# A reciprocal on VectorE in place of an exponential and two products, with the order of a planned kernel worked out anew

## The chip, the cores and the metric

The kernel runs on one core of one Trainium2 chip. The metric is device time in microseconds (us). The engines are TensorE (PE in the profile, with PEld for its weight loads), VectorE (DVE), ScalarE (ACT), GpSimd (POOL) and SyncE (SP, which issues the DMAs). They run beside each other, each works through its own list of instructions strictly in order, and they wait for each other by semaphores.

## The reference

A linear attention with a complex decay per step, followed by a two-layer network with a softplus. Sizes are batch B=4, heads H=8, sequence S=768, head dimension D=48, d_model 384, d_ff 2048; all fp32.

```
mag = sqrt(a_re^2 + a_im^2);  scale = min(mag, 0.999) / (mag + 1e-6)
for t in range(S):                       # per batch and head, S_re and S_im are D x D
    S_re, S_im = ar*S_re - ai*S_im + k_t v_t^T,  ar*S_im + ai*S_re      # (ar, ai) = a*scale
    y[t] = q_t . S_re
x = y, as B*S tokens of 384
out = softplus(x @ w_in) @ w_out
```

The kernel before does not step through t. It takes the logarithm of the decay: log(mag) from log(a_re) and 0.5*log(1 + r^2), and the angle from arctan(r), where **r = a_im/a_re** is the ratio of the decay's two parts. Both are summed along the sequence, and q and k are multiplied by exp(+-sum), cos and sin, so that chunks of 128 steps become matmuls.

## The kernel before

The sequence is cut into 6 groups of 128 steps, a group has 4 chunks (one for each batch), 24 chunks in all. The decay's work (the function `pre`) is done in 14 slices: slices 0 to 3 are one chunk of group 0 each, 128x384 elements; slices 4 to 13 are two chunks each, 128x768 elements. For a slice, `pre` lists these steps in this order:

- DMAs bring a_re, a_im (`x`, the parts `re()` and `im()`) and q, k into one buffer.
- L466 to L471 make the ratio r in `v3`: on ScalarE `v1 = Ln(re)` and `v2 = Exp(-v1)`, which is 1/re to the precision of two table functions, and on VectorE three products, the last two of which correct it: `im = im*v2`, `v3 = re*v2`, `v3 = (v3 - 2)*im`. This is -r, so that the arctan further down takes it with scale -1.
- L473 to L481 make log(mag) with its cap, on ScalarE (Square, Ln, Exp, Ln) and VectorE (L476, L481).
- The running sums along the sequence: in slices 0 to 3 by a matmul with a triangular mask (`sums`, L507), in the others by VectorE's scan (`scan`, L486 to L493). Then exponentials (L525, L526), the product with q and k (L530), arctan (L532), angles (L545, L547), sine and cosine (L535 to L537) and two products with q and k (`tail`, L563, L565).

For each chunk, `chunk` moves q and k into the layout `qk` by DMA, transposes k (L621, L628, L630), computes scores (L646), masks them on VectorE (L649), multiplies by v and by the state (L677, L680) and splits the result y in two fp32r parts, high `xt0` (L688 on VectorE or L689 on ScalarE) and low `xt1` (L690, VectorE). `kv` (L701) and L707 to L710 update the state.

The network (`moe`) runs for 512 tokens of one group and 128 columns of d_ff at a time, in 96 such steps. A step is nine matmuls into `h` (L736), on ScalarE Abs, Exp and Ln (L741 to L743), on VectorE `lt = max(h,0) + lt` (L744), a high part `gh` (L746 on VectorE or L747 on ScalarE, whichever the planner picks), a low part `gl` (L748, VectorE), and, two steps later in the list, nine matmuls into three `o` accumulators (L760). Two buffers `h`, two `lt` and six `g` lie between the engines. The weights are converted from words of 64 bits on VectorE and ScalarE (L350 to L367).

The order of all this is not written by hand. Every step is added to a `Planner` with an engine, a duration that the planner assumes, and a key; `order` then plays the engines through with these assumed durations, and at each moment takes the step with the lowest key that is ready. The keys come from a table of numbers `K`. Steps with an alternative (`gh`, `xt0`, copies of `o`, some conversions) go to the engine that the planner finds free. Where TensorE would have nothing to do before the first `o` matmul is planned, the planner puts in filler matmuls (L796) whose result is not used. The assumed durations are formulas, for example:

```
def d1(n):
    return n / 960 + 0.066
def a1(n, ap=0):
    return n / 1200 + 0.1 + 0.09 * ap
```

Of the kernel before, what the change touches and what calls it, by code (L numbers as in the profile page):

```python
# [15 lines left out]
AF = mybir.ActivationFunctionType  # L16
ALU = mybir.AluOpType
# [67 lines left out]
class Planner:  # L85
# [29 lines left out]
    def add(self, eng, dur, fn, key, r=(), w=(), tab=None, nbytes=0):  # L115
        t = Task(eng, dur, fn, key, len(self.tasks), tab, nbytes)
        self.tasks.append(t)
        seen = set()
        for accs, wr in ((r, False), (w, True)):
            for a in accs:  # L120
                buf, part = a if isinstance(a, tuple) else (a, None)
                for e in buf.hist:
                    if (part is None or e[0] is None or e[0] == part) and (wr or e[2]) and e[1] is not t:
                        t.deps.add(e[1])
                if wr and part is None:
                    buf.hist = []
                buf.hist.append((part, t, wr))
                if buf not in seen:
                    seen.add(buf)
                    buf.users += 1  # L130
                    t.bufs.append(buf)
        return t
# [128 lines left out]
def d1(n):  # L261
    return n / 960 + 0.066
# [6 lines left out]
def a1(n, ap=0):  # L269
    return n / 1200 + 0.1 + 0.09 * ap  # L270
# [6 lines left out]
class Prog:  # L277
# [119 lines left out]
    def pre(self, si):  # L397
        nc = self.nc
        V, A, PE = nc.vector, nc.scalar, nc.tensor
        add = self.plan.add  # L400
# [3 lines left out]
        W = n * CH  # L404
# [9 lines left out]
        if first:  # L414
            ra, ia, sa = [(x, (z, 0))], [(x, (z, 2))], [(x, (z, 1))]
        else:
            ra, ia, sa = [(x, (0, 0))], [(x, (1, 0))], [(x, (0, 1)), (x, (1, 1))]
# [3 lines left out]
        if first:  # L421
            t = Buf(self.wpool, f"w{'io'[si % 2]}{NWP - 1 - si // 2}", [P, 2 * NI * WCOL], F32R, f"t_{si}")
            t1, t2, t3 = (((t, j), lambda j=j: t()[:, j * W : (j + 1) * W].bitcast(F32)) for j in range(3))
            t4, t5 = t2, t1
        else:
            t1, t2, t3, t4, t5 = ((z, lambda z=z: z()[:, :W]) for z in
                                  (Buf(p, "t", [P, 2 * NI * CH], F32, f"t{j}_{si}", NT) for j in range(1, 6)))
# [4 lines left out]
        def region(j):  # L432
            return x().rearrange("p (c j n) -> p c j n", c=2, j=2)[:, z : z + m, j]

        if first:
            re = lambda: region(0)[:, 0, :W]
            im = lambda: region(0)[:, 0, W:]
        else:
            re = lambda: region(0)[:, 0]
            im = lambda: region(0)[:, 1]  # L440
# [6 lines left out]
        col = lambda j: chk[:, 2 * si + j : 2 * si + j + 1]  # L447
# [3 lines left out]
        def at(part="head"):  # L451
            step[0] += 1
            return K[part][si] + step[0] * 0.05
# [6 lines left out]
        for c in range(m):  # L460
# [2 lines left out]
            add("SP", 0.45, lambda vt=vt, gc=gc: nc.sync.dma_start(vt(), self.vpad[:, gc, :]),  # L463
                K["chunk"][gc] - K["vlead"], w=[vt], nbytes=4 * VW * P)

        add("ACT", a1(W), lambda: A.activation(v1(), re(), AF.Ln), at(), r=ra, w=[t1], tab="log")  # L466
        add("ACT", a1(W, 1), lambda: A.activation(v2(), v1(), AF.Exp, scale=-1.0, accum_out=col(0)),
            at(), r=[t1], w=[t2, (self.flags, 2 * si)], tab="log")
        add("DVE", d1(W), lambda: V.tensor_tensor(im(), im(), v2(), ALU.mult), at(), r=[t2], w=ia)
        add("DVE", d1(W), lambda: V.tensor_tensor(v3(), re(), v2(), ALU.mult), at(), r=[t2] + ra, w=[t3])  # L470
        add("DVE", d1(W), lambda: V.scalar_tensor_tensor(v3(), v3(), 2.0, im(), ALU.subtract, ALU.mult),  # L471
            at(), r=ia, w=[t3])
        add("ACT", a1(W, 1), lambda: A.activation(re(), v3(), AF.Square, accum_out=col(1)),  # L473
            at(), r=[t3], w=ra + [(self.flags, 2 * si + 1)])
        add("ACT", a1(W, 1), lambda: A.activation(re(), re(), AF.Ln, bias=self.one), at(), w=ra, tab="log")
# [45 lines left out]
        else:  # L521
            lb, vl = t1, v1
            add("DVE", st, lambda: scan(0, v1, v1), at(), r=[car[0]],
                w=[t1] + ([(self.flags, (0, si))] if last else [car[0]]))
# [4 lines left out]
            keep(0, lb, vl, at())  # L529
        add("DVE", d1(2 * W), lambda: V.tensor_tensor(region(1), region(1), region(0), ALU.mult), at(), r=ca, w=sa)  # L530
        def arctan():
            A.activation(v3(), v3(), AF.Arctan, scale=-1.0)  # L532

        def sincos():
            A.activation(v4(), v3(), AF.Sin, scale=TURN)  # L535
# [22 lines left out]
        def tail():  # L558
            h = NI * 2 * CH
            for c in range(m):  # L560
# [5 lines left out]
                    at("tail"), r=[t4], w=r1)  # L566

        return (arctan, a1(W), [t3]), (sincos, 2 * a1(W) + a1(W, 1) + 0.28, [t4, t3]), turn, tail

    def trig(self, key, *parts):  # L570
# [384 lines left out]
    def tokens(self):  # L955
# [75 lines left out]


K = {
    "judge": 1000000.0,
    "head": [
        274.27, 191.42, -19.05, 1886.88, -522.94, 3908.76, 1353.27, 120.66, 663.62, 2137.45, 3530.29,
        1964.06, 1785.73, 1014.39,
    ],
    "turn": [
        -811.22, 2808.33, 895.09, 2597.24, -283.88, 1643.47, 2180.8, 1352.75, 1602.08, 2955.2, 3052.45,  # L1040
        2418.74, 2757.83, 1578.39,
    ],
    "tail": [
        -2437.59, 1540.19, -1353.87, 2017.89, -135.23, 668.85, 932.44, 944.77, 145.34, 194.8, 232.6,
        1598.99, 1138.83, 2676.38,
    ],
    "chunk": [
        -689.49, -686.77, 740.28, 1628.59, 1541.82, 611.66, 1299.05, 1015.66, 1529.3, 1799.41, 3880.02,
        3677.37, 1662.92, 1429.47, 2231.74, 1027.09, 2317.51, 356.29, 1181.0, 2433.8, 429.57, 324.71,
        492.66, 2147.0,  # L1050
    ],
    "state": [
        -865.61, -1248.14, -159.16, -396.04, 43.1, 43.1, 90.73, 46.85, 128.01, 128.32, 139.34, 139.15,
        154.61, 198.54, 235.65, 212.71, 254.45, 273.15, 303.36, 280.34, 880.92, 864.29, 16.84, 1017.82,
    ],
    "wgt": [
        -474.48, -2074.48, -586.01, -122.47, -914.3, 393.73, -1500.13, 949.7, 1718.07, 1958.85, 814.56,
        993.07, 2739.59, 1078.09, 309.09, 77.07,
    ],
    "moe": [  # L1060
        38.3, 81.85, 155.32, 196.13, 296.48, 341.98, 532.78,
    ],
    "step": [
        4.721, 3.356, 1.527, 6.239, 2.402, 18.243, 113.085,
    ],
    "seen": 258.893,
    "seenstep": 56.443,
    "rlead": -1133.562,
    "xlead": -906.378,
    "vlead": 57.841,  # L1070
    "plead": -233.471,
    "backlog": 1.833,
    "altpen": -0.192,
    "tpen": 10.673,
    "table": 1.3,
}

# [61 lines left out]
```

## Time and profile before

| | |
|---|---|
| median of 3 runs | 598.09 us (597.23 to 829.45) |
| the profiled execution, its own time | 598.15 us |
| its span, first to last instruction | 596.4 us |
| TensorE busy | 577.3 us (97%) |
| VectorE busy | 439.0 us (74%) |
| ScalarE busy | 437.3 us (73%) |
| granted TensorE clock | 0.997 |

The page gives busy times over the whole span, and these are averages over an opening, in which slices are prepared and TensorE runs mostly filler, and a long stretch in which the network's matmuls run. A busy TensorE may be running filler: the 328 records of L796 are the 164 filler instructions, each recorded as two passes, and they hold TensorE for 39.8 us.

### The profile page before, as it was taken

What the parts mean: (1) busy time and instruction counts of PE and PEld (TensorE: products, weight loads), DVE (VectorE), ACT (ScalarE), POOL (GpSimd) and SP (SyncE); (2) the same over time, 40 slices, a digit from 0 to 9 for tenths busy, and PEclk for the clock granted to TensorE, in tenths of its full rate; (3) what the DMA queues carried; (4) which work ended last, traced back from release to release, by engine and by line L of the source; (5) the groups of instructions that cost most, each with busy time, mean ns of one, the idle gap of its engine ahead of it and who ended that gap; (6) DMA issues with size and microseconds to landing.
All of it is one profiled execution on the core that took longest, in us unless ns stands there. A gap on an engine that the chain in (4) does not pass through costs nothing.

```text
span 596.4 us, 10864 instructions
## 1 busy us (share of the span) xinstructions
PE 577.3 (97%) x4338; PEld 487.0 (82%) x4338; DVE 439.0 (74%) x678; ACT 437.3 (73%) x768; POOL 1.8 (0%) x16
## 2 busy tenths in 40 slices
PE   1999999999999999999999999999999999999995
PEld 1999988888878888888888888887888888888884
DVE  6999999998998989777876985979336643533442
ACT  7987587847988695948859769687458834569982
POOL 1000000000000000000000000000000000000000
PEclk9999999999999999999999999999999999999998
DMA  8899843404004345515440435414105600057712
GB/s 324 343 301 276 316 123 123 123 27 165 0 1 106 124 114 183 138 53 159 102 143 28 130 129 130 144 51 106 43 1 158 175 2 1 1 153 243 217 50 57
DMA packets 42232, 75.47 MB, mean 127 GB/s; under 512 B 3520, under 2 KB 26560, under 8 KB 42176
## 3 DMA queue, kind: packets, MB, share of 16 engines
q1 hardware_dynamic: 42176, 74.73, 41.1%
q8 instruction: 35, 0.57, 0.4%
q14 instruction: 21, 0.17, 0.1%
HBM read 50.33 MB, written 5.51 MB: 94 GB/s over the span
## 4 chain that ended last, share of the span: by engine, by line
PE 80%; DVE 7%; ACT 7%; DMA 2%; SPq 1%; issue 1%; ACTq 0%; DVEq 0%
PE o L760 29%; PE h L736 28%; PE o L796 6%; PE sc L646 6%; PE kv L701 3%; PE y L680 3%; PE y L677 2%; PE tr L621 1%; DMA x<-dense_dram 1%; ACT L848 1%; DVE lt L744 1%; PE sum L507 1%; SPq L606 1%; ACT lt L742 1%; DVE gl L748 1%
## 5 line engine op out<-in xcount | busy, mean ns | idle before, releaser
L736 PE MATMUL h<-xt,wi 128*128 128x512 f32 x864 | 217.5, 397 | 0.2
L760 PE MATMUL o<-gh,wo 128*128 128x512 f32 x576 | 198.2, 400 | 0.0
L736 PEld LDWEIGHTS h<-xt,wi 128*128 128x128 f32 x864 | 159.7, 188 | 36.3 <-DVE lt L744 1.0
L744 DVE SCALAR_TENSOR_TENSOR lt<-h,lt 128x512 f32<-128x512 f32 x96 | 66.0, 688 | 93.1 <-ACT lt L743 92.9
L760 PEld LDWEIGHTS o<-gh,wo 128*128 128x128 f32 x576 | 108.4, 188 | 25.9 <-issue 1.8
L760 PE MATMUL o<-gl,wo 128*128 128x512 f32 x288 | 113.6, 395 | 0.0
L741 ACT ACTIVATE lt<-h 128x512 f32<-128x512 f32 x96 | 56.7, 592 | 77.1 <-PE h L736 74.0
L743 ACT ACTIVATE lt<-lt,one 128x512 f32<-128x512 f32 x96 | 69.2, 721 | 1.9
L748 DVE TENSOR_TENSOR gl<-lt,gh 128x512 fp32r<-128x512 f32 x96 | 66.2, 689 | 5.7 <-ACT gh L747 3.6
L760 PEld LDWEIGHTS o<-gl,wo 128*128 128x128 f32 x288 | 54.3, 188 | 11.5 <-DVE gl L748 0.4
L742 ACT ACTIVATE lt<-lt 128x512 f32<-128x512 f32 x96 | 60.4, 629 | 1.9
L646 PE MATMUL sc<-qk 96*128 96x128 f32 x384 | 49.1, 278 | 0.5 <-DVE xt L690 0.4
L646 PEld LDWEIGHTS sc<-qk 96*128 96x128 f32 x384 | 46.7, 192 | 2.8 <-PE sc L646 0.6
L649 DVE TENSOR_TENSOR a<-sc,mask 128x512 f32<-128x512 f32 x48 | 32.2, 684 | 12.6 <-PE sc L646 12.6
L796 PE MATMUL o<-ident 128*128 128x128 f32 x328 | 39.8, 278 | 0.0
L796 PEld LDWEIGHTS o<-ident 128*128 128x128 f32 x328 | 38.5, 194 | 0.2 <-issue 0.2
L747 ACT ACTIVATE gh<-lt 128x512 fp32r<-128x512 f32 x38 | 23.9, 629 | 19.8 <-DVE lt L744 16.5
L490 DVE TENSOR_TENSOR_SCAN t<-hold,t 128x384 f32<-128x384 bf16 x40 | 36.1, 945 | 1.2 <-DMA out_dram<-o 0.3
L848 ACT ACT_TABLE_LOAD x28 | 35.9, 1283 | 0.4
L701 PEld LDWEIGHTS kv<-v,kt 128*96 128x96 f32 x320 | 29.6, 165 | 2.0 <-ACT kt L628 0.5
L701 PE MATMUL kv<-v,kt 128*96 128x64 f32 (+1 forms) x320 | 29.7, 246 | 0.0
L563 DVE TENSOR_TENSOR x<-x,t 128x768 f32<-128x768 f32 x24 | 22.0, 952 | 10.6 <-ACT t L537 10.4
(88 smaller groups left out, 617.5 us busy)
## 6 DMA issues: line engine op xcount, KB each, us to landing
x<-dense_dram SPq DMA_DIRECT2D x20, 768.0 KB, 5.9
qk<-x SPq DMA_DIRECT2D x48, 288.0 KB, 4.2
raw_wo<-w_out_dram SPq DMA_DIRECT2D x8, 768.0 KB, 9.0
raw_wi<-w_in_dram SPq DMA_DIRECT2D x8, 768.0 KB, 10.1
seen<-w_in_dram SPq DMA_DIRECT2D x16, 384.0 KB, 3.8
seen<-w_out_dram SPq DMA_DIRECT2D x16, 384.0 KB, 3.7
v<-vpad_dram SPq DMA_DIRECT2D x24, 224.0 KB, 2.6
qk<-x SPq DMA_DIRECT2D x48, 96.0 KB, 3.8
```

The lines of the kernel that those rows point to most:

```text
L490: V.tensor_tensor_scan(out()[:, s], self.hold, inc()[:, s], 0.0, ALU.mult, ALU.add)
L646: PE.matmul(psc()[:, hh * P : (hh + 1) * P], q[:, h, CH:], q[:, h, :CH], start=True, stop=True)
L701: PE.matmul(kv()[: 2 * D, s], k[:, 2 * D * h : 2 * D * (h + 1)], v[:, s], start=h == 0, stop=h == H - 1)
L736: PE.matmul(h()[:, :n], w()[:, q, i, fs], x()[:, i, :n], start=k == 0, stop=k == 3 * NI - 1)
L741: add("ACT", a1(n) - 0.04, lambda: A.activation(tv(), h(), AF.Abs), k, r=[h], w=[t])
L742: add("ACT", a1(n), lambda: A.activation(tv(), tv(), AF.Exp, scale=-1.0), k, w=[t], tab="log")
L743: add("ACT", a1(n, 1), lambda: A.activation(tv(), tv(), AF.Ln, bias=self.one), k, w=[t], tab="log")
L744: add("DVE", d1(n), lambda: V.scalar_tensor_tensor(tv(), h(), 0.0, tv(), ALU.max, ALU.add), k, r=[h], w=[t])
L748: add("DVE", d1(n), lambda: V.tensor_tensor(gl(), tv(), gh().bitcast(F32), ALU.subtract), k, r=[t, gh], w=[gl])
L760: PE.matmul(acc[m]()[:, :n], w()[:, wq, f % 2, ms], x(), start=f == f0 and q == 0, stop=f == f1 - 1 and q == 2)
L796: self.nc.tensor.matmul(self.acc0[0]()[:, :P], self.ident, x, start=True, stop=True)
L848: nc.scalar.preload_act_table_set(TABLES[table])
```

## The change

In `pre`, 1/re comes from VectorE's reciprocal instruction and is multiplied once by im. The Exp and two of the three products go. The Ln of re stays, since log(mag) needs it; it moves behind the two VectorE steps in the list, and it now carries the sum over columns (`accum_out`) that the Exp carried. The ratio has its natural sign, so the arctan loses its scale of -1. The planner assumes `d1(W)` for the reciprocal, the same as for a product. From L466 on, line numbers of the changed kernel are lower by 3 (L744 becomes L741), except within the changed lines.

```diff
-        add("ACT", a1(W), lambda: A.activation(v1(), re(), AF.Ln), at(), r=ra, w=[t1], tab="log")
-        add("ACT", a1(W, 1), lambda: A.activation(v2(), v1(), AF.Exp, scale=-1.0, accum_out=col(0)),
-            at(), r=[t1], w=[t2, (self.flags, 2 * si)], tab="log")
-        add("DVE", d1(W), lambda: V.tensor_tensor(im(), im(), v2(), ALU.mult), at(), r=[t2], w=ia)
-        add("DVE", d1(W), lambda: V.tensor_tensor(v3(), re(), v2(), ALU.mult), at(), r=[t2] + ra, w=[t3])
-        add("DVE", d1(W), lambda: V.scalar_tensor_tensor(v3(), v3(), 2.0, im(), ALU.subtract, ALU.mult),
-            at(), r=ia, w=[t3])
+        add("DVE", d1(W), lambda: V.reciprocal(v2(), re()), at(), r=ra, w=[t2])
+        add("DVE", d1(W), lambda: V.tensor_tensor(v3(), im(), v2(), ALU.mult), at(), r=ia + [t2], w=[t3])
+        add("ACT", a1(W, 1), lambda: A.activation(v1(), re(), AF.Ln, accum_out=col(0)),
+            at(), r=ra, w=[t1, (self.flags, 2 * si)], tab="log")
...
-            A.activation(v3(), v3(), AF.Arctan, scale=-1.0)
+            A.activation(v3(), v3(), AF.Arctan)
...
 K = {
...
     "head": [
-        274.27, 191.42, -19.05, 1886.88, -522.94, 3908.76, 1353.27, 120.66, 663.62, 2137.45, 3530.29,
...
+        -189.5437767, -1095.6183614, 1348.051687, 4369.562575, -1151.1824664, 4502.4467243, 1094.3014723,
...
-    "altpen": -0.192,
-    "tpen": 10.673,
+    "altpen": 1.1854543,
+    "tpen": 0.0,
```

All the keys in `K` are new, so all engines' lists are in another order. Counted over the whole list, `gh` is now made on VectorE 87 times and on ScalarE 9 times (58 and 38 before), the high part of y on VectorE 15 times and ScalarE 9 (8 and 16), copies of `o` on VectorE never and on ScalarE 18 times (7 and 11). There are 149 fillers (164 before). The list still has 28 table loads on ScalarE.

VectorE's list at the start of the program, where slices 0 and 1 (buffer `x_98`, work tiles `t_105` and `t_110`) and slice 2 (`x_101`, `t_116`) are begun, before:

```order
L469 TENSOR_TENSOR x_98<-x_98,t_105 128x384
L470 TENSOR_TENSOR t_105<-x_98,t_105 128x384
L471 SCALAR_TENSOR_TENSOR t_105<-t_105,x_98 128x384
L469 TENSOR_TENSOR x_98<-x_98,t_110 128x384
L470 TENSOR_TENSOR t_110<-x_98,t_110 128x384
L471 SCALAR_TENSOR_TENSOR t_110<-t_110,x_98 128x384
L469 TENSOR_TENSOR x_101<-x_101,t_116 128x384
L476 SCALAR_TENSOR_TENSOR t_105<-x_98,t_105 128x384
```

The same place now, with `t_111` for slice 1, `t_117` for slice 2 and `t_126` for slice 3:

```order
L466 RECIPROCAL t_105<-x_98 128x384
L467 TENSOR_TENSOR t_105<-x_98,t_105 128x384
L466 RECIPROCAL t_111<-x_98 128x384
L467 TENSOR_TENSOR t_111<-x_98,t_111 128x384
L466 RECIPROCAL t_117<-x_101 128x384
L467 TENSOR_TENSOR t_117<-x_101,t_117 128x384
L473 SCALAR_TENSOR_TENSOR t_105<-x_98,t_105 128x384
L466 RECIPROCAL t_126<-x_101 128x384
```

Seven products stood ahead of slice 0's L476, and three of them (L469) wait for an Exp of ScalarE. Now three reciprocals and three products stand there, and they wait only for the data; slice 0's L476 (now L473) comes behind all three pairs.

VectorE's list some 280 rows in, where slice 8 (`x_8`) is begun while the network's steps run, with all numbers in the names, before:

```order
L744 SCALAR_TENSOR_TENSOR lt_2026<-h_1978,lt_2026 128x512
L469 TENSOR_TENSOR x_8_1949<-x_8_1949,t2_8_2066 128x768
L470 TENSOR_TENSOR t3_8_2075<-x_8_1949,t2_8_2066 128x768
L690 TENSOR_TENSOR xt1_2_2089<-y8_1992,xt0_2_2053 128x3x128
L649 TENSOR_TENSOR a9_0_2091<-sc9_0_2070,mask_63 128x512
L471 SCALAR_TENSOR_TENSOR t3_8_2075<-t3_8_2075,x_8_1949 128x768
L744 SCALAR_TENSOR_TENSOR lt_2077<-h_2056,lt_2077 128x512
L746 TENSOR_SCALAR gh_2102<-lt_2026 128x512
L748 TENSOR_TENSOR gl_2113<-lt_2026,gh_2102 128x512
```

The same place now:

```order
L646 TENSOR_TENSOR a8_1_2071<-sc8_1_2049,mask_63 128x512
L466 RECIPROCAL t2_8_2073<-x_8_1912 128x768
L741 SCALAR_TENSOR_TENSOR lt_2056<-h_2034,lt_2056 128x512
L467 TENSOR_TENSOR t3_8_2111<-x_8_1912,t2_8_2073 128x768
L685 CAST xt0_2_2115<-y9_1940 128x3x128
L687 TENSOR_TENSOR xt1_2_2119<-y9_1940,xt0_2_2115 128x3x128
L707 TENSOR_TENSOR s0_322<-s0_322,kv8_1979 96x448
L685 CAST xt0_2_2115<-y8_2075 128x3x128
L741 SCALAR_TENSOR_TENSOR lt_2109<-h_2060,lt_2109 128x512
L687 TENSOR_TENSOR xt1_2_2119<-y8_2075,xt0_2_2115 128x3x128
L743 TENSOR_SCALAR gh_2151<-lt_2056 128x512
L745 TENSOR_TENSOR gl_2153<-lt_2056,gh_2151 128x512
```

Here too three products between the network's steps have become one reciprocal and one product, and behind the reciprocal stand the `lt` of a network step (row L741), the parts of y for group 2 and the `gh` and `gl` of that step.

More of the change, by code (lines that the diff above doesn't have):

```diff
@@ L1033 @@
 K = {
-    "judge": 1000000.0,
+    "judge": 996922.8115805,
     "head": [
-        274.27, 191.42, -19.05, 1886.88, -522.94, 3908.76, 1353.27, 120.66, 663.62, 2137.45, 3530.29,
-        1964.06, 1785.73, 1014.39,
+        -189.5437767, -1095.6183614, 1348.051687, 4369.562575, -1151.1824664, 4502.4467243, 1094.3014723,
+        111.6437803, 1466.2076468, 2500.7966242, 3749.465863, 1724.6099285, 530.2549858, 4709.0997584,
     ],
     "turn": [
-        -811.22, 2808.33, 895.09, 2597.24, -283.88, 1643.47, 2180.8, 1352.75, 1602.08, 2955.2, 3052.45,
-        2418.74, 2757.83, 1578.39,
+        -588.517208, 2703.7351482, -115.5964185, 902.3216395, -261.2865587, 2048.659054, 3301.4083645,
+        5666.0129994, 1591.9111595, 6817.500403, 5139.1219234, 3203.3417137, 6650.5823943, 7876.9779079,
@@ L1042 @@
     ],
     "tail": [
-        -2437.59, 1540.19, -1353.87, 2017.89, -135.23, 668.85, 932.44, 944.77, 145.34, 194.8, 232.6,
-        1598.99, 1138.83, 2676.38,
+        -3289.9856183, 1542.7509828, -1659.2146031, 2151.3903496, 1194.1306982, 1077.6737751, 918.1437842,
+        1336.8579015, 1245.1778233, 1065.1191328, 1843.262914, 904.2955969, 1581.1640849, 3609.1259645,
     ],
     "chunk": [
-        -689.49, -686.77, 740.28, 1628.59, 1541.82, 611.66, 1299.05, 1015.66, 1529.3, 1799.41, 3880.02,
@@ L1049 @@
-        3677.37, 1662.92, 1429.47, 2231.74, 1027.09, 2317.51, 356.29, 1181.0, 2433.8, 429.57, 324.71,
-        492.66, 2147.0,
+        -994.0129508, -858.8235624, 2667.3083537, 1712.33123, 1826.2698824, 1922.6270186, 2361.0881931,
+        2333.8096342, 2862.8859902, 4415.5035231, 1382.4751648, 5870.4794199, 4247.1233368, 1075.8988181,
+        4641.737538, 3771.4577794, 3661.2283634, 3681.7292081, 2801.1050397, 4820.1886287, 896.6722344,
+        350.6727813, 904.3629076, 1830.6785783,
     ],
@@ L1052 @@
     "state": [
-        -865.61, -1248.14, -159.16, -396.04, 43.1, 43.1, 90.73, 46.85, 128.01, 128.32, 139.34, 139.15,
-        154.61, 198.54, 235.65, 212.71, 254.45, 273.15, 303.36, 280.34, 880.92, 864.29, 16.84, 1017.82,
+        -1724.787855, -1321.9409719, -95.5677617, -478.8731411, 44.5817511, 44.6430058, 97.5374477,
+        46.539593, 124.4192676, 124.0906646, 134.2244832, 133.8406669, 171.1899725, 171.0439535,
+        226.8421803, 188.0533859, 264.3168775, 284.5608017, 289.0636233, 311.9269159, -363.3893295,
@@ L1055 @@
+        -36.3179112, 2341.3166356, -1144.4893667,
     ],
     "wgt": [
-        -474.48, -2074.48, -586.01, -122.47, -914.3, 393.73, -1500.13, 949.7, 1718.07, 1958.85, 814.56,
-        993.07, 2739.59, 1078.09, 309.09, 77.07,
+        -1034.6616942, -1688.8160235, -3117.2077214, 477.5148695, -1191.568273, 528.4463301, -1963.4590907,
+        141.7678986, 3228.4011287, 3461.8424897, 4100.686858, 4784.7762647, 5096.0676908, 3688.5211343,
+        1108.1101094, 646.1807584,
     ],
     "moe": [
-        38.3, 81.85, 155.32, 196.13, 296.48, 341.98, 532.78,
+        40.7197473, 91.5028147, 123.5077092, 342.4434914, 346.7917168, 683.3761671, 1265.1098621,
@@ L1062 @@
     ],
     "step": [
-        4.721, 3.356, 1.527, 6.239, 2.402, 18.243, 113.085,
+        1.3073878, 2.5087282, 4.8729526, 0.3547812, 19.025501, 47.8605307, 265.4619385,
     ],
[L1066 to L1072, printed above, removed]
-    "altpen": -0.192,
-    "tpen": 10.673,
+    "seen": 254.220629,
+    "seenstep": 17.062814,
+    "rlead": -1276.1206566,
+    "xlead": -1132.5226652,
@@ L1075 @@
+    "vlead": -1051.2875511,
+    "plead": -1488.3307859,
+    "backlog": 1.7468005,
+    "altpen": 1.1854543,
+    "tpen": 0.0,
     "table": 1.3,
```

## The prediction

> **What bounds the kernel now.** I read the page's shares and slices first, then what TensorE waited for, then the busy times of stretches, then the rows of the operations that change.
>
> ```profile
> PE 577.3 (97%) x4338; PEld 487.0 (82%) x4338; DVE 439.0 (74%) x678; ACT 437.3 (73%) x768; POOL 1.8 (0%) x16
> PE   1999999999999999999999999999999999999995
> DVE  6999999998998989777876985979336643533442
> ACT  7987587847988695948859769687458834569982
> PE 80%; DVE 7%; ACT 7%; DMA 2%; SPq 1%; issue 1%; ACTq 0%; DVEq 0%
> PE sum L507 <- DVE t L481: 12.1, 1, 12.1
> L796 PE MATMUL o<-ident 128*128 128x128 f32 x328 | 39.8, 278 | 0.0
> ```
>
> TensorE is busy in every slice but the first and the last, and it is 80% of the chain that ended last. Its only long wait is for the first running sums (L507), 12.1 us for VectorE's L481. VectorE is the second limit: over the first two thirds of the span its digits are 7 to 9. So a change that takes work off VectorE or ScalarE can win little, and one that adds work to VectorE meets little room. The stretches say how little:
>
> ```profile
> core 0: us, PE busy (x) PEld busy (x) DVE busy (x) ACT busy (x) POOL busy (x), PEclk, DMA share, GB/s
> 0.00:77.00 77.00, 64.95 (x659) 63.53 (x660) 69.35 (x113) 59.88 (x109) 1.76 (x16) 1.00 0.88 305
> 0.00:260.00 260.00, 247.14 (x2127) 215.27 (x2128) 236.06 (x362) 202.26 (x345) 1.76 (x16) 1.00 0.51 163
> 260.00:412.00 152.00, 151.89 (x1191) 126.70 (x1191) 117.38 (x177) 116.11 (x196) 0.00 (x0) 1.00 0.38 110
> 73.91 2.72 PE L796 MATMUL o<-ident 128*128 128x128 f32 x22
> 76.39 3.92 PE L736 MATMUL h<-xt,wi 128*128 128x512 f32 x16
> ```
>
> In the first 77 us, up to the first network matmul at 76.39 us, VectorE is idle for 7.65 us and TensorE runs filler: the opening belongs to VectorE. Up to 260 us VectorE is idle for 24 us in all; from 260 to 412 us for 35 us. From 76.39 us on TensorE hardly pauses, so the end is the opening plus a fixed amount of matmuls.
>
> **The change part by part.** The rows of the steps that go, and of the nearest others on VectorE:
>
> ```profile
> L466 ACT ACTIVATE t<-x 128x768 f32<-128x768 f32 x10 | 8.4, 842 | 7.3 <-DMA x<-dense_dram 7.3
> L467 ACT ACTIVATE t<-t 128x768 f32<-128x768 f32 x10 | 8.4, 839 | 0.8 <-DMA out_dram<-o 0.7
> L469 DVE TENSOR_TENSOR x<-x,t 128x768 f32<-128x768 f32 x10 | 9.5, 954 | 4.7 <-ACT t L467 4.6
> L470 DVE TENSOR_TENSOR t<-x,t 128x768 f32<-128x768 f32 x10 | 9.5, 950 | 0.0
> L471 DVE SCALAR_TENSOR_TENSOR t<-t,x 128x768 f32<-128x768 f32 x10 | 9.5, 950 | 0.0
> L470 DVE TENSOR_TENSOR t<-x,t 128x384 f32<-128x384 f32 x4 | 2.2, 550 | 0.0
> L490 DVE TENSOR_TENSOR_SCAN t<-hold,t 128x384 f32<-128x384 bf16 x40 | 36.1, 945 | 1.2 <-DMA out_dram<-o 0.3
> L746 DVE TENSOR_SCALAR gh<-lt 128x512 fp32r<-128x512 f32 x58 | 24.7, 425 | 4.0
> L747 ACT ACTIVATE gh<-lt 128x512 fp32r<-128x512 f32 x38 | 23.9, 629 | 19.8 <-DVE lt L744 16.5 <-PE o L760 3.0
> ```
>
> *ScalarE* loses one Exp in each slice, 10 x 0.84 us and about 4 x 0.5 us, 10 us in all; with the 29 gh that move to VectorE (29 x 0.63 = 18 us) it is relieved by some 28 us. TensorE's list of waits above names ScalarE nowhere, so I count this at nothing.
>
> *VectorE's products.* Each slice loses two products: 2 x 0.95 us in a large one, 2 x 0.55 us in a small one.
>
> *The reciprocal* does not occur in the trace, and it decides the case. The least it can take is one pass over the elements, as a product does: 0.95 and 0.55 us, with 1.04 ns for each further element ((950 - 550)/384) and 0.15 us fixed. The scan row shows that not every VectorE instruction runs at one pass: 945 ns for 384 elements is two passes by that slope. The other end is what a division costs if it is made of products: one step of refinement is the pair L470 and L471, 1.90 us at 768 elements, and doubles the correct digits. From a start with two or three bits, 24 bits take three to four steps, up to eight products, 7.6 us at 768 elements. A division is nearer in kind to that correction, which the kernel so far does by hand, than to a single product. I take one pass for a start value and three steps of two, **seven passes inside one instruction**: 0.15 + 7 x 0.80 = 5.75 us for 768 elements and 2.95 us for 384. Both ends stay in the range. [...]
>
> *Summed at a mark.* I take the 31st `gl` (L748), since its place in VectorE's list is known for both kernels, and so is what TensorE still has to do behind it.
>
> ```profile
> 0.00:259.00 259.00, 21.09 (x31) 1.00 0.52 163
> 258.51 0.68 DVE L748 TENSOR_TENSOR gl<-lt,gh 128x512 fp32r<-128x512 f32 x1
> 589.86 0.40 PE L760 MATMUL o<-gh,wo 128*128 128x512 f32 x1
> 60.84 1.48 PE L701 MATMUL kv<-v,kt 128*96 128x64 f32 x16
> 62.16 2.02 PE L646 MATMUL sc<-qk 96*128 96x128 f32 x16
> 53.47 0.84 PE L621 MATMUL tr<-ident,x 128*128 128x128 f32 x6
> 72.90 1.08 PE L680 MATMUL y<-a,v 128*32 128x128 f32 x32
> ```
>
> Before, the mark is reached at 259.2 us with 235 us of VectorE's work, and TensorE ends at 590.26 us, 331 us later. In the new list the same mark has ahead of it:
> - four small and six large reciprocals: 4 x 2.95 + 6 x 5.75 = 46.3 us;
> - 8 small and 12 large products fewer: 4.4 + 11.4 = 15.8 us less;
> - 16 more gh on VectorE, 6.8 us, against four scans (3.8 us), three copies of o and some ten small things fewer: together 1.5 us less.
>
> That is 29 us more, 264 us of VectorE's work. To it comes its idle time, between the opening's 7.65 us, which are waits for the first DMAs and the first sums and stay, and the 24 us of before, most of which was waiting for TensorE and goes when VectorE is late; I take 16 us. The mark is then at 280 us instead of 259. Behind it the new order leaves TensorE one chunk more (96 score matmuls instead of 88): the rows above, 1.48 + 2.02 + 0.84 and twice 1.08 us, overlapping by some tenths, are 6 us. So TensorE has 337 us left, and 280 + 337 = 617 us.
>
> *Behind the mark*, up to the 57th gl (412 us before), VectorE has 117 + 28 = 145 us of work (117 is before's row; the 28 are four more reciprocals less eight products, 15 us, five more gh, 2 us, and scans, masks and casts that stood ahead of the mark and now stand behind it, 11 us) against some 162 us of TensorE's. So TensorE leads again on average, but each reciprocal holds VectorE's queue for 5.75 us, while TensorE has only about two network steps at hand: behind the reciprocal of slice 8 stand the `lt`, `gh` and `gl` that the next `o` matmuls need. A pair of steps is 4.2 us of TensorE by the rows below, so each of the four costs it about 1.5 us, 6 us in all.
>
> ```profile
> 560.76 2.08 PE h L736 x9
> 562.84 2.09 PE o L760 x9
> ```
>
> That gives 623 us for TensorE's end. From there to the end of the span it is 6.1 us (596.4 - 590.26), the copies and DMAs of the last outputs, which the change leaves; and the profiled execution lasts 1.75 us longer than its span (598.15 against 596.4), which is the median of the runs within 0.1 us. **Sum: 631 us**, by rounding 632.
>
> *What is counted at nothing.* The first chain to L507 gets no Exp and no wait for ScalarE but three reciprocals in VectorE's queue ahead of L476; its difference is inside the idle time. The fillers fall by 15, 15/164 of 39.8 us, 3.6 us: they are only what TensorE does while it waits for VectorE, and would come back as plain waiting. SP's queue issues the same loads in another order; in the opening its DMA share is 0.88, and I leave that inside the same allowance.
>
> **The rivals.**
>
> *The reciprocal takes one pass* (not slower). Then VectorE has 6 x 4.8 + 4 x 2.4 = 38 us less by the mark than in my sum, 9 us less than before, TensorE is the bound from its first network matmul on, and the time comes from the opening: four small slices save 4 x 0.55 us of products there, the first chain loses two ScalarE steps of some 0.5 us, and 3.6 us of filler go; but gh, taken off ScalarE, eats VectorE's gain later. That is 5 us less than before, 593 us. For it speaks that every other row of VectorE in the trace but the scan keeps to one pass. [...] It decides from two passes down: each pass is 6 x 0.80 + 4 x 0.40 = 6.4 us at the mark, so (631 - 598)/6.4 = 5 passes fewer than seven give the time of before.
>
> *Two to four passes*, as the scan has two: 598 to 612 us, mostly within 2% of before.
>
> *The new order itself* is worse or better than the old one with measured durations, whatever the reciprocal takes. It moves 29 gh (12 us) and 7 high parts of y (4 us) to VectorE, and takes 7 copies of o (5 us) off it. By the counts above that is within 2 us at the mark; I put 5 us to either side.
>
> **How the numbers follow.** A measurement of this kernel can tell about 2% from no change, 12 us here. Five passes and more: 0.67, all slower by over 2%, its own range 610 to 648 us (five passes with the lower idle time, to 7.6 and 4.4 us for each reciprocal, which adds 17 us). Two to four passes: 0.07, mostly within 2%. One pass: 0.26, 588 to 598 us; of that 0.02 are faster by over 2%, if the opening gains over 12 us. Leaving out the one-pass case would leave out more than 2 in 10, so the range goes from 590 to 647 us. Faster 0.02, same 0.30, slower 0.68.
>
> **What would show it.** A row RECIPROCAL with a mean near 5.7 us at 128x768 and 2.9 us at 128x384; VectorE busy for some 490 us (439 and 55), at 9 tenths up to two thirds of the span; TensorE waiting for L741 or L745 behind reciprocals, some 25 us in all ahead of 300 us; the first network matmul some 5 to 10 us later. If the row says about 0.9 us, the term is wrong by 38 us and the time near 593 us. If the row is as I say and the time is still near 600 us, then the idle time or the slack of TensorE was misjudged.

## The result and the profile after

The changed kernel takes **648.97 us** (median of 4 runs, 648.26 to 653.88) against 598.12 us for the kernel before: ratio 1.0871, 95% interval 1.0842 to 1.0901. It is slower by 51 us. One of the four runs of the kernel before took 829.45 us and is left out of the ratio; such slow runs turn up with several of the kernels. The forecast was 632 us with a range up to 647: the direction was right, and so was the cause that it named, a reciprocal of several passes; the size was not.

The page of the changed kernel, in the lines that answer to those of before: busy times, the slices of the span, and the chain that ended last.

```profile
span 646.8 us, 10793 instructions
PE 591.4 (91%) x4308; PEld 494.9 (77%) x4308; DVE 486.2 (75%) x692; ACT 416.9 (64%) x726; POOL 1.8 (0%) x16
PE   0997899898999999799899979997999999999996
DVE  7989989799998997978988897696634764444442
PEclk9998999899899999999999999998999999999999
PE 37%; ACT 4%; DVE 3%; issue 2%; DMA 1%
```

VectorE is busy for 486.2 us instead of 439.0. TensorE's row now has 7s and 8s up to two thirds of the span, and in places the granted clock dips with them; its mean is 0.978 against 0.997 before. The first network matmul comes at 87.83 us, 11.4 us later than before. The chain line can't be set against the 80% of before: its shares add up to 47% of the span, since the profile follows the chain back only to 342.94 us, and within it TensorE has 37 parts of 47. The groups by line and shape (busy us, mean ns of one) name the cause, and the list of TensorE's waits (us in total, times, longest) its effect:

```profile
L466 DVE RECIPROCAL t<-x 128x768 f32<-128x768 f32 x10 | 49.4, 4945 | 0.0
L466 DVE RECIPROCAL t<-x 128x384 f32<-128x384 f32 x4 | 10.2, 2547 | 4.1 <-DMA x<-dense_dram 4.1
L467 DVE TENSOR_TENSOR t<-x,t 128x768 f32<-128x768 f32 x10 | 9.5, 950 | 0.1
PE sum L504 <- ACT t L529: 16.5, 1, 16.5
PE y L674 <- DVE a L646: 6.7, 2, 3.7
PE tr L618 <- DVE x L562: 6.4, 4, 3.5
PE h L733 <- DVE lt L741: 5.9, 3, 3.8
PE o L757 <- DVE gh L743: 4.6, 2, 2.4
```

The reciprocal takes 4.945 us for 768 elements and 2.547 us for 384: 6.24 ns for each further element, where a product's slope was 1.04 by the rows of before. That is the time of **six passes**; what the engine does in it no run shows. What TensorE waited for is VectorE in every line but the first, which is the first running sum.

One such place, in the timeline of VectorE and of TensorE (start, duration, and in brackets the idle time before it):

```profile
154.92 0.69 DVE L741 SCALAR_TENSOR_TENSOR lt<-h,lt 128x512 f32<-128x512 f32 x1
155.53 4.94 DVE L466 RECIPROCAL t<-x 128x768 f32<-128x768 f32 x1
160.39 0.36 DVE L743 TENSOR_SCALAR gh<-lt 128x512 fp32r<-128x512 f32 x1
156.07 2.34 PE L733 MATMUL h<-xt,wi 128*128 128x512 f32 x9
160.81 0.80 PE L757 MATMUL o<-gh,wo 128*128 128x512 f32 x1 [2.40 <-DVE gh L743]
161.93 0.80 PE L757 MATMUL o<-gl,wo 128*128 128x512 f32 x1 [0.32 <-DVE gl L745]
162.52 1.05 PE L757 MATMUL o<-gh,wo 128*128 128x512 f32 x2
168.91 0.62 PE L757 MATMUL o<-gh,wo 128*128 128x512 f32 x2
```

This reciprocal of a large slice stands between a network step's `lt` and its `gh` and holds VectorE for 4.94 us. TensorE has one `h` of work meanwhile and then waits for 2.40 us. Its next matmuls take 0.80 us each, and pairs 1.05 us, where 6 us later a pair takes 0.62 us. The busy times by stretches have the granted clock in the last column but two:

```profile
150.00:160.00 10.00, 8.31 (x46) 6.35 (x43) 9.75 (x8) 5.72 (x11) 0.00 (x0) 1.00 0.54 180
160.00:170.00 10.00, 8.87 (x25) 6.73 (x26) 9.76 (x16) 5.96 (x11) 0.00 (x0) 0.66 0.01 2
170.00:180.00 10.00, 10.00 (x44) 8.11 (x44) 8.61 (x14) 7.85 (x12) 0.00 (x0) 1.00 0.00 0
161.00:167.00 6.00, 5.68 (x13) 4.12 (x14) 6.00 (x11) 4.66 (x8) 0.00 (x0) 0.50 0.01 3
167.40:167.60 0.20, 0.20 (x3) 0.16 (x2) 0.20 (x2) 0.00 (x0) 0.00 (x0) 1.00 0.00 0
```

The clock is 0.66 in the 10 us behind the pause and 1.00 before and after. In finer stretches it is 0.50 from 160.6 to 167.2 us: after the pause TensorE is slow for some 7 us. For most of that time it is busy, 5.68 of the 6 us from 161 to 167 us. Not every pause has such a stretch behind it: from 243 to 247 us, at a pause of 2.20 us that ends at 243.25 us, the clock is 1.00, and from 273 to 276 us, behind a pause of 3.68 us, it is 0.53.

### The profile page after: what moved, and what is told of

The parts are those of the page before. It is cut to its first block, busy times and chain, and to the rows that moved or that the text cites. A ratio compares the mean times of both kernels' runs of the same rounds, so it can differ in the third digit from the quotient of the medians.

```text
span 646.8 us, 10793 instructions
## 1 busy us (share of the span) xinstructions
PE 591.4 (91%) x4308; PEld 494.9 (77%) x4308; DVE 486.2 (75%) x692; ACT 416.9 (64%) x726; POOL 1.8 (0%) x16
## 5 line engine op out<-in xcount | busy, mean ns | idle before, releaser
L733 PE MATMUL h<-xt,wi 128*128 128x512 f32 x864 | 220.7, 401 | 6.0 <-DVE lt L741 5.9
L757 PE MATMUL o<-gh,wo 128*128 128x512 f32 x576 | 200.8, 405 | 4.6 <-DVE gh L743 4.6
L733 PEld LDWEIGHTS h<-xt,wi 128*128 128x128 f32 x864 | 162.1, 191 | 44.0 <-DVE lt L741 7.0
L741 DVE SCALAR_TENSOR_TENSOR lt<-h,lt 128x512 f32<-128x512 f32 x96 | 66.0, 688 | 100.0 <-ACT lt L740 99.5
L757 PEld LDWEIGHTS o<-gh,wo 128*128 128x128 f32 x576 | 109.8, 191 | 32.2 <-DVE gh L743 5.5
L757 PE MATMUL o<-gl,wo 128*128 128x512 f32 x288 | 114.9, 399 | 0.6 <-DVE gl L745 0.6
L740 ACT ACTIVATE lt<-lt,one 128x512 f32<-128x512 f32 x96 | 69.6, 725 | 2.2
L466 DVE RECIPROCAL t<-x 128x768 f32<-128x768 f32 (+1 forms) x14 | 59.6, 4260 | 4.1 <-DMA x<-dense_dram 4.1
L743 DVE TENSOR_SCALAR gh<-lt 128x512 fp32r<-128x512 f32 x87 | 36.9, 424 | 4.9
L793 PE MATMUL o<-ident 128*128 128x128 f32 x298 | 37.2, 283 | 0.0
L793 PEld LDWEIGHTS o<-ident 128*128 128x128 f32 x298 | 36.2, 201 | 0.2 <-issue 0.2
L470 ACT ACTIVATE x<-t 128x768 f32<-128x768 f32 (+1 forms) x14 | 10.5, 751 | 38.8 <-issue 35.4
## 6 DMA issues: line engine op xcount, KB each, us to landing
qk<-x SPq DMA_DIRECT2D x48, 288.0 KB, 4.3
```

Source lines behind the costliest of these rows:

```text
L466: add("DVE", d1(W), lambda: V.reciprocal(v2(), re()), at(), r=ra, w=[t2])
L733: PE.matmul(h()[:, :n], w()[:, q, i, fs], x()[:, i, :n], start=k == 0, stop=k == 3 * NI - 1)
L740: add("ACT", a1(n, 1), lambda: A.activation(tv(), tv(), AF.Ln, bias=self.one), k, w=[t], tab="log")
L741: add("DVE", d1(n), lambda: V.scalar_tensor_tensor(tv(), h(), 0.0, tv(), ALU.max, ALU.add), k, r=[h], w=[t])
L743: x = add("DVE", d2(n), lambda: V.tensor_scalar(gh(), tv(), 1.0, None, ALU.mult), k, r=[t], w=[gh])
L757: PE.matmul(acc[m]()[:, :n], w()[:, wq, f % 2, ms], x(), start=f == f0 and q == 0, stop=f == f1 - 1 and q == 2)
```

## Experiments

The question was first whether the reciprocal's duration is the whole loss or the new order has a part in it, and then why the loss is larger than the sum that was made for it.

### One pass in place of the reciprocal, same order

This kernel leaves out the division: a single instruction that only scales re stands in the reciprocal's place.

```diff
-        add("DVE", d1(W), lambda: V.reciprocal(v2(), re()), at(), r=ra, w=[t2])
+        add("DVE", d1(W), lambda: V.scalar_tensor_tensor(v2(), re(), 1.0 / 51.84, re(), ALU.mult, ALU.min), at(), r=ra, w=[t2])
```

> The changed kernel with its order, row for row, but in place of each reciprocal a single VectorE instruction that scales re by 1/51.84 (0.55 and 0.95 us expected); the ratio is then only approximate. Theory A (the reciprocal's 48 us beyond one pass on VectorE are the whole loss, and pauses of TensorE add to them): 588 to 598 us, TensorE without waits after its first network matmul. Theory B (the new order is itself worse than the old one): over 605 us. The prediction's own one-pass rival said 593 us.

Measured: 597.17 us, ratio to the kernel before 1.0003 (0.9987 to 1.0020). The page:

```profile
span 595.1 us, 10793 instructions
PE 575.4 (97%) x4308; PEld 483.0 (81%) x4308; DVE 438.3 (74%) x692; ACT 414.5 (70%) x726; POOL 1.8 (0%) x16
L793 PE MATMUL o<-ident 128*128 128x128 f32 x298 | 35.5, 275 | 0.0
71.56 4.43 PE L733 MATMUL h<-xt,wi 128*128 128x512 f32 x18
```

With a single pass in this place the new order is no worse than the old one, and no better: theory B falls. Everything by which the changed kernel is slower comes, in this order, with the reciprocal's duration, 59.6 us of VectorE against 11.7 us of the single passes, 47.9 us more. The prediction's one-pass rival said 593 us, which was 4 us too low: the first network matmul does come 4.8 us earlier (71.56 against 76.39), but in the profiled executions only 1.3 us of it reach the end of the span, and in the medians nothing that stands clear of the noise. In these two profiles filler falls by 4.3 us, the other matmuls' busy time grows by 2.4 us (575.4 - 35.5 against 577.3 - 39.8), and the idle time by 0.6 us.

### True reciprocals in some slices only

```diff
+        add("DVE", d1(W), (lambda: V.reciprocal(v2(), re())) if si < 4 else (lambda: V.scalar_tensor_tensor(...)), ...
```

with `si < 4` (early), `3 < si < 10` (mid) and `si > 9` (late), each in the changed kernel's order. All three leave out the division in the other slices.

> As e1_onepass, but the true reciprocal in slices 0 to 3, the four small ones of the opening (2.55 us each, 8 us beyond one pass in all). If the opening belongs to VectorE, all 8 us are paid: e1_onepass plus 7 to 10 us, first network matmul that much later. If they hide behind DMAs and ScalarE there: plus 0 to 3 us.

> As e1_onepass, but the true reciprocal in slices 10 to 13 only, the four large ones behind the prediction's mark (4 x 4.0 = 16 us beyond one pass). By the prediction (1.5 us of TensorE for each, the rest hidden by VectorE's slack): e1_onepass plus 4 to 7 us. Theory A with pauses (VectorE's queue is held, TensorE runs dry, and then runs slower for some microseconds): plus 14 to 22 us. If slack hides them altogether: plus 0 to 2 us.

> As e1_onepass, but the true reciprocal in slices 4 to 9, the six large ones that the prediction's sum put ahead of its mark (6 x 4.0 = 24 us beyond one pass). If the parts simply add up (after less e1_onepass 52 us, e2_early 7 us, e3_late 16 us): e1_onepass plus 28 to 30 us, 626 us. If each microsecond is paid once and no more: plus 24 us, 621 us. If VectorE's backlog from the opening makes the middle ones worse in the changed kernel than alone: plus 15 to 22 us.

Measured: 604.14, 613.42 and 626.89 us, ratios 1.0105 (1.0081 to 1.0128), 1.0267 (1.0250 to 1.0284), 1.0498 (1.0452 to 1.0545). What they add to VectorE and to the time, by the RECIPROCAL rows and medians:

| reciprocals in | more on VectorE | more time than one pass |
|---|---|---|
| slices 0 to 3 | 8.0 us | 7.0 us |
| slices 10 to 13 | 16.0 us | 16.3 us |
| slices 4 to 9 | 24.0 us | 29.7 us |
| all (the changed kernel) | 47.9 us | 51.8 us |

The parts add up, 53.0 against 51.8 us, and in this order each microsecond put on VectorE is paid, early, mid or late, the mid ones at 1.24 us each. The early ones move the first network matmul from 71.56 to 79.14 us, the mid ones to 83.02: part of the loss is there before the network starts. The late ones settle the point that the prediction had left to VectorE's slack: four reciprocals cost 16.3 us, not 6. From the page of the late ones, with TensorE's waits:

```profile
span 609.3 us, 10793 instructions
PE 578.4 (95%) x4308; PEld 485.5 (80%) x4308; DVE 454.3 (75%) x692; ACT 415.1 (68%) x726; POOL 1.7 (0%) x16
PE h L733 <- DVE lt L741: 6.7, 3, 3.8
```

TensorE's idle time is 609.3 - 578.4 = 30.9 us, 11.2 us more than with one pass, and its busy time grows by 3.0 us. The first are pauses; that the second are slower matmuls behind them is likely, but not shown in this run.

### Three passes

```diff
-        add("DVE", d1(W), lambda: V.reciprocal(v2(), re()), at(), r=ra, w=[t2])
+        add("DVE", d1(W), lambda: [V.scalar_tensor_tensor(...) for _ in range(3)], at(), r=ra, w=[t2])
```

> As e1_onepass, but the one-pass instruction three times in a row (some 2.8 us at 768 elements, 1.6 us at 384; 23 us more VectorE work in all). By the prediction's slope of 6.4 us for each pass: e1_onepass plus 13 us. If every microsecond of VectorE is paid: plus 22 to 27 us. If there is a threshold, since queues hide holds as short as 2.8 us: plus 0 to 6 us.

Measured: 619.21 us, ratio 1.0369 (1.0343 to 1.0396). Three passes cost 23.7 us of VectorE beyond one (35.4 against 11.7), and 22.0 us of time. A hold of VectorE's queue for some 2.8 us is not hidden, and the slope is not 6.4 us for a pass: it is 11 us.

With these runs one number stands out. The page's first lines (span, and VectorE's busy time) give **VectorE's idle time**, and it is nearly the same in all of them:

| | span | VectorE busy | VectorE idle |
|---|---|---|---|
| before | 596.4 | 439.0 | 157.4 |
| one pass | 595.1 | 438.3 | 156.8 |
| early | 602.4 | 446.3 | 156.1 |
| late | 609.3 | 454.3 | 155.0 |
| three passes | 616.3 | 461.6 | 154.7 |
| mid | 625.0 | 462.3 | 162.7 |
| after | 646.8 | 486.2 | 160.6 |

What VectorE waits for does not change either; its longest wait in total, with one pass and in the changed kernel:

```profile
DVE lt L741 <- ACT lt L740: 96.1, 47, 5.2
DVE lt L741 <- ACT lt L740: 99.5, 51, 5.2
```

The sum over the span does not say where this idle time lies. Cut at the 31st and at the 57th `gl` (to 1 us), the two kernels with the same order compare like this:

| VectorE | one pass: us, busy, idle | changed kernel: us, busy, idle |
|---|---|---|
| up to the 31st `gl` | 253.0, 226.4, 26.6 | 288.0, 258.0, 30.0 |
| from there to the 57th | 162.0, 127.1, 34.9 | 177.0, 143.2, 33.8 |
| behind it | 180.1, 84.9, 95.2 | 181.8, 85.0, 96.8 |

Some 95 us of the idle time lie behind the last reciprocal, where VectorE's work is the same and nothing had to be paid. What counts are the first two rows: 32 and 16 us of work went in, and the idle time there did not shrink to make room for it. The constant belongs to this order. It is 156.5 us with the halves below, in the same order, but 140.5 us after a new search for keys, 176.9 us when the planner is told with the old keys, and 174.4 us with less work in the order of before. That the kernel before, with an order of its own, has 157.4 us is not explained.

### Each reciprocal in two halves

```diff
+        def recip(j):
+            s = slice(j * W // 2, (j + 1) * W // 2)
+            V.reciprocal(v2()[:, s], re()[:, s])
+        def ratio():
+            recip(1)
+            V.tensor_tensor(v3(), im(), v2(), ALU.mult)
+        add("DVE", d1(W), lambda: recip(0), at(), r=ra, w=[t2])
+        add("DVE", d1(W), ratio, at(), r=ia + [t2], w=[t3])
```

> The changed kernel with its order, but each reciprocal is two instructions of half the columns: the first at the reciprocal's place, the second right ahead of the product that follows it in VectorE's list. In the large slices one to six rows of other steps (a lt, a mask, a gh) stand between the two, so that VectorE's queue is held for 2.6 us and then again for 2.6 us instead of 5 us at once; the total work is the same. If the length of the hold is what makes TensorE run dry: 10 to 25 us below the changed kernel's 649. If VectorE's total work is what counts: 646 to 653 us.

Measured: 644.86 us, ratio 1.0809 (1.0778 to 1.0840) against 1.0871 for the changed kernel. The work stays (20 halves of 2537 ns in the large slices), the hold is half as long, and 4 us of 52 come back: between the two expectations, nearer to the second. Halving the hold brings little, at these lengths; the work is the large part.

### The planner told the truth

```diff
-        add("DVE", d1(W), lambda: V.reciprocal(v2(), re()), at(), r=ra, w=[t2])
+        add("DVE", W * 0.00624 + 0.15, lambda: V.reciprocal(v2(), re()), at(), r=ra, w=[t2])
```

with the changed kernel's keys; then in four pieces; then with keys found by a new search for the true duration.

> The changed kernel with its keys, but the planner is told what the reciprocal takes (6.24 ns for each element and 0.15 us), so that it can place it and the steps around it accordingly; 88 gh stay on VectorE. If the loss comes from an order that was planned for a short reciprocal: 600 to 625 us. If it comes from VectorE's total work: 638 to 652 us.

> As e5_told, but each reciprocal is four instructions of a quarter of the columns, four steps of the planner's list, so that VectorE's queue is held for 1.3 us at a time instead of 5 us. If the hold of the queue is what costs (TensorE runs dry behind it): 10 us or more below e5_told. If only the total work counts: within 4 us of e5_told, on either side.

> True reciprocals everywhere; the planner is told what they take and its keys are searched anew for that. Against the changed kernel this leaves VectorE the same 48 us beyond one pass but gives the order a chance to put them where they wait for nobody and to move gh back to ScalarE. If the loss is only the order's ignorance: 597 to 605 us. If VectorE is simply too full ahead of the last slices: 615 to 630 us. If a search for keys changes nothing: 645 us or more.

Measured: 661.35 us, 663.63 us and 620.77 us; ratios 1.1066 (1.1033 to 1.1099), 1.1102 (1.1069 to 1.1135) and 1.0403 (1.0380 to 1.0426). The first run misses both of its expectations. Told the truth but with keys that were searched for another duration, the planner makes a worse order than the one made in ignorance; the second run therefore tells nothing on holds, since its order is again another. With keys searched for the true duration, 28 us come back and 23 us stay. The page of the last:

```profile
span 617.7 us, 11050 instructions
PE 591.5 (96%) x4438; PEld 498.3 (81%) x4438; DVE 477.2 (77%) x671; ACT 423.4 (69%) x747; POOL 1.8 (0%) x16
L793 PE MATMUL o<-ident 128*128 128x128 f32 x428 | 50.8, 276 | 0.0
90.88 4.44 PE L733 MATMUL h<-xt,wi 128*128 128x512 f32 x18
```

TensorE's pauses are nearly gone (idle 26.2 us, 19.1 before), and the larger part of the loss stands in the opening: the first network matmul comes at 90.88 us instead of 76.39.

### The other way round: less work on VectorE

The Exp stays and two products go, which leaves the Exp's own error in the ratio; the arctan loses its scale of -1. First the two steps are taken out of the planner's list as well, which with the kernel before's keys gives a new order; then, as in the lines below, the planner keeps their places, with the old order row for row, and last with every sixth filler left out as well.

```diff
-        add("DVE", d1(W), lambda: V.tensor_tensor(im(), im(), v2(), ALU.mult), at(), r=[t2], w=ia)
-        add("DVE", d1(W), lambda: V.tensor_tensor(v3(), re(), v2(), ALU.mult), at(), r=[t2] + ra, w=[t3])
-        add("DVE", d1(W), lambda: V.scalar_tensor_tensor(v3(), v3(), 2.0, im(), ALU.subtract, ALU.mult), ...)
+        add("DVE", d1(W), lambda: None, at(), r=[t2], w=ia)
+        add("DVE", d1(W), lambda: V.tensor_tensor(v3(), im(), v2(), ALU.mult), at(), r=[t2] + ra, w=[t3])
+        add("DVE", d1(W), lambda: None, at(), r=ia, w=[t3])
```

> No reciprocal: ScalarE's Ln and Exp as in the kernel before and its keys, but only the one product im * Exp(-Ln re); the two products that correct the Exp's error are left out, 28 VectorE instructions, some 23 us. If VectorE's work in the opening still sets the time: 4 x 2 x 0.55 us less, 592 to 595 us. If TensorE's matmuls take back what the opening gives, as in e1_onepass: 596 to 599 us.

> The kernel before in its own order, with the Exp, but only one product im * Exp(-Ln re): the two correcting products are taken out of VectorE's list, 28 instructions, and nothing else moves. If VectorE sets the length of the opening: 4 x 2 x 0.55 = 4.4 us less, 593 us. If TensorE's list sets it, since its 164 fillers are executed whether they are needed or not: only the first running sum comes earlier, by 1 to 2 us, 595.5 to 597 us.

> As e11_drop_two, and every sixth filler is left out, 27 of 164 (27 x 0.24 = 6.6 us of TensorE's opening). If the fillers are what keeps the freed VectorE time from being used: 3 to 6 us below e11_drop_two. If VectorE or the DMAs set the opening after all: equal to e11_drop_two, with waits of TensorE in place of the fillers. If the pauses make TensorE slower afterwards: above e11_drop_two.

Measured: 620.82 us, 1.0377 (1.0333 to 1.0421); 595.95 us, 0.9973 (0.9964 to 0.9982); 594.95 us, 0.9952 (0.9937 to 0.9966). The same arithmetic is 23 us slower or 1.6 us faster than before, by the order alone; the slower run lies above both of its expectations. In the old order 18.7 us less on VectorE (420.3 against 439.0) bring 1.6 us:

```profile
span 594.7 us, 10837 instructions
PE 576.6 (97%) x4338; PEld 487.9 (82%) x4338; DVE 420.3 (71%) x650; ACT 437.5 (74%) x768; POOL 1.8 (0%) x16
L795 PE MATMUL o<-ident 128*128 128x128 f32 x328 | 39.8, 278 | 0.0
76.53 4.40 PE L735 MATMUL h<-xt,wi 128*128 128x512 f32 x18
```

The first network matmul does not move (76.53 against 76.39), and TensorE executes its 39.8 us of filler whether VectorE needs the time or not. Without 27 of the fillers, 6.2 us of TensorE, it comes at 74.56 us, 2.0 us earlier, and the median falls by another 1.0 us instead of the 3 to 6 expected, though the two intervals touch. So the fillers hold the opening only in part; what holds the rest of it stays open. These two are the only versions that beat both kernels.

## Why the prediction was right and wrong

**Right:** that the reciprocal's duration decides; that it takes several passes and not one; that TensorE would wait for `lt` and `gh` behind it; that what ScalarE gains counts for nothing. The first network matmul was said to come 5 to 10 us later, and comes 11.4 us later. VectorE's work up to the 31st `gl` was summed to 264 us, of which 6 us were the price of a seventh pass. The stretches of the changed kernel, up to that mark and on to the 57th:

```profile
0.00:288.00 288.00, 252.17 (x2008) 216.98 (x2009) 258.04 (x354) 187.40 (x316) 1.76 (x16) 0.96 0.44 141
288.00:465.00 177.00, 163.80 (x1358) 135.54 (x1357) 143.15 (x194) 127.08 (x231) 0.00 (x0) 0.98 0.47 140
```

It is 258 us: the counting of rows was right. So were the 337 us that TensorE has left at the mark: in the one-pass kernel, with the same order, they are 336 us.

**The term that was too large:** seven passes, 5.75 and 2.95 us, for 4.945 and 2.547 measured. The seven were a guess from a division made of products, and no run shows a division made that way. By itself this makes the sum 6 us too long at the mark, and 3 us behind it, where each late reciprocal was priced at its length less 4.2 us. With the true price the sum of 631 us (the forecast of 632 rounds it up) would have been 622 us, and missed by 27.

**The step that failed: VectorE's idle time up to the mark.** I took 16 us, on the argument that most of the 24 us of before "was waiting for TensorE and goes when VectorE is late". It is 288 - 258 = 30 us, more than the 24 of before; this is 14 of the 27 us. The list of VectorE's waits does not bear the premise out. The three longest waits up to 259 us in the kernel before, and behind them the three up to 288 us in the changed one (us in total, times, longest), are:

```profile
DVE x L469 <- ACT t L467: 7.1, 3, 5.5
DVE x L563 <- ACT t L537: 5.1, 4, 2.1
DVE lt L744 <- ACT lt L743: 3.8, 6, 1.8
DVE x L560 <- ACT t L534: 6.8, 4, 2.4
DVE lt L741 <- ACT lt L740: 5.9, 7, 2.1
DVE t L466 <- DMA x<-dense_dram: 4.1, 1, 4.1
```

Before, the list names ScalarE for 20.4 us and TensorE for 0.8 us; it gives only the last link, and some of ScalarE's steps had in turn waited for TensorE, those ahead of `lt` for `h`. Of the opening's 7.65 us, too, 6.2 us end with the Exp that the change removes, and not with the first DMAs and sums; the 4.1 us for a DMA stand in their place now. In the changed kernel the waits for sine and cosine (L534) and for the network (L740) have not gone; in the one-pass kernel they are 6.4 and 4.4 us, so 32 us of reciprocals left them where they were. A likely reason is that VectorE waits there for things made from its own earlier results, so that what holds VectorE holds them too: the angles go to ScalarE and come back as sine and cosine, and `h`, three steps on ScalarE, `lt`, `gh`, `gl` and `o` form a loop through short queues. This is argued from the order of the steps; no run takes one of these waits away.

**The second step that failed: four reciprocals behind the mark at 1.5 us each.** From the mark at 287 us to TensorE's last matmul at 640.4 us it is 353 us, where I had 337 + 6, and would have had 337 + 3 with the true price: the other 13 us. The late reciprocals measured alone cost 16.3 us instead of 6. I had let VectorE's average slack there (145 us of work in 162) hide most of each hold. The slack is there, but the table by stretches shows it untouched: 34 us idle with the reciprocals and 35 without. And more is lost than the length of TensorE's pauses: against one pass in the same order, TensorE's idle time grows by 35.7 us (55.4 against 19.7) and the busy time of its matmuls other than filler by 14.3 us (554.2 against 539.9). The mean granted clock, 0.978 of 646.8 us against 0.997 of 595.1, gives an estimate of 12 us of full clock lost between the two, most of the 14.3. Both are read from the profiles; no run takes the slow stretches away alone.

**The rivals.** The one-pass case was priced at 593 us, with a range of 588 to 598, and measures 597. It had taken the opening's gain for the end's. The two-to-four-pass case was priced at 598 to 612 us, and three passes measure 619, with the slope wrong for the same reasons as above. That the new order costs at most 5 us either way held where a single pass stands in the reciprocal's place. With the true reciprocal the order counts for more: the new search for keys takes 28 us off it.

## What to carry to other kernels

Where two engines feed each other through short queues and both are nearly full, and the order stays as it is, price an addition to the engine that the other waits for at its full length, wherever it stands, and do not pay it from that engine's other waits: in the changed kernel's order VectorE's idle time stayed at 155 to 163 us while its work grew by 48. A new search for an order that knows the true duration got 28 of the 52 us back. A saving does not count in the same way: 18.7 us less on VectorE brought 1.6 us. And a table of searched keys belongs to the steps and durations it was searched with: change either, and search again, or keep the order and delete in place.

## What the hardware showed that was not expected

VectorE's reciprocal runs at 6.24 ns for each element (4.945 us at 768, 2.547 us at 384), six times the slope of a product, with the same 0.15 us fixed. After a pause of 2.40 us TensorE's granted clock was 0.50 for some 7 us, and its matmuls of 512 columns came at 0.43 us apiece instead of 0.23.
